# Turning batch 0's later keys and queries on TensorE, with three small reorderings, in a top-k attention and shrink kernel

## The chip, the cores and the metric

The kernel runs on one core of a Trainium2 chip. The metric is the device time of one launch in microseconds (us), the median of several executions. Engines are named as in the profile: PE is TensorE (matmuls; PEld is its weight loads), DVE is VectorE, ACT is ScalarE, POOL is GpSimd, SP is SyncE, which here only issues DMAs.

## The reference

```python
def _attn_ref(q, k, v):                       # (8, 8, 576, 64), float32
    B, H, S, D = q.shape
    scale = 1.0 / np.sqrt(D)
    scores = scale * np.matmul(q, k.transpose(0, 1, 3, 2))
    kth = np.partition(scores, -32, axis=-1)[..., -32:-31]
    mask = scores >= kth
    scores = np.where(mask, scores, -1000000000.0)
    scores = scores - np.max(scores, axis=-1, keepdims=True)
    attn = np.exp(scores)
    attn = attn / (np.sum(attn, axis=-1, keepdims=True) + 1e-09)
    return np.matmul(attn, v).astype(np.float32)

def _moe_ref(x, w_in, w_out):                 # x: (4608, 512); w_in: (512, 2048); w_out: (2048, 512)
    h = x @ w_in
    g = h - np.tanh(h)
    return (g @ w_out).astype(np.float32)
```

The attention output, heads side by side, is the input `x` of the second block. `w_in` and `w_out` come as 64-bit floats, and the kernel makes 32-bit floats of them on the chip.

## The kernel before, in words

**Steps.** Attention goes in steps of 128 queries of two heads (a pair `hp`). Batch 0 comes first. Its first four steps (0 to 3) are query tile 0 of pairs 0, 1, 2 and 3, so each of them needs a new pair's keys and queries. Batch 0's steps are marked `pe`: their attention weights are turned by PE (`turn_pe`, L423), later batches' by DVE and DMAs.

**One iteration n** of the main loop (`run`, from L708) emits, in program order: `turn_pe(n-2)`'s first part (eight PE transposes L423 into `zt`, two ACT copies L426 into `et`); `mask(n-1)`; `search(n)`; `scores(n+1)` (PE L236, ACT copy L244 from `scps` to `sc`); the last part of `turn_pe`; `expo(n-1)` (ACT L329); `values` (PE L451 and L461, ACT L465, POOL L469); and, dealt out in between by a planner, the matmuls of the second block (`ffn_h`, PE L502, with ACT L514/L515 and POOL L516; `ffn_o`, PE L523). Every engine works through its own list in that order. The planner counts steps, not time, so what is dealt to which step is fixed in the program.

**`search(n)`, on DVE:** L266, L267, L269 split the 576 scores of each row into two halves (min, max) and then run four rounds of MAX8 (L274) and MATCH_REPLACE8 (L277; not after the last round). After round i it calls `between(i)`, which emits whatever was put at (n, i): turning of keys (round 0), stages of weight conversion, and the reciprocal L345.

**`mask(n)`, on POOL and ACT:** L293 makes the threshold `tb`, L302 `nb`, then twice ACT L306 and POOL L309 make the masked scores `z`; last comes L313, which notes in `bad` whether a row needs an exact repeat. L313 reads the buffer `ab` that `search` filled.

**Weight conversion.** A piece is 128 rows by 512 weights; there are 32, pieces 0 to 15 of `w_in`, 16 to 31 of `w_out`. `convert` has a load (two SP DMAs, L148 the words and L149 the same bytes shifted) and two further stages. Stage 1: DVE L157 (exponent bits to `f`), ACT L160 (exponent `e`), DVE L162 and ACT L165 (mantissa). Stage 2: DVE L168 puts the sign to the exponent, POOL L171 multiplies; the piece's load buffer is then free, and the next load is issued behind it. For `w_in` `e` is a tile of `h_ps`, a PSUM pool of two buffers that the second block's matmuls use too; for `w_out` `e` is `f` itself, in SBUF. Steps 0 and 1 have two pieces each, steps 2 to 9 three, step 10 four (`many`). Their stages are spread over a step's rounds:

```python
for i, x in enumerate(seq):      # x = (stage, piece), as 1k 1k+1 2k 1k+2 2k+1 2k+2 for three pieces
    at_round.setdefault((m, 3 * i // max(len(seq) - 1, 1)), []).append(lambda x=x: part(*x))
```

**Keys and queries.** `load_rows` brings a pair's keys or queries with four DMAs of 32 partitions by 18 runs of 32 floats (L199), so that one DVE 32 by 32 block transpose (L221, `turn_rows`) gives the turned matrix `kT` or `qT`. Pair 0 of batch 0 goes to tiles of its own; three of its query DMAs are on ACT's queue, all other loads on SP's. Pairs 1 to 3 of batch 0 are loaded at the start into the space of `w_in[2]` and `w_in[3]` (`early`) and turned in round 0 of steps 0, 1 and 2. On SP the loads stand in the order pair 0, piece 0, pair 1, piece 1, pair 2, piece 2, pair 3, piece 3, then three more pieces and the values `v` (L211, L215).

**Pools that matter here:** `sc` 3 buffers, `ab` 2, `z` 2, `sc_ps` (the scores in PSUM) 1, `zt_ps` 2, `h_ps` 2, `th` (which holds `f`) 4.

Of the kernel before, what the change touches and what calls it, by code (L numbers as in the profile page):

```python
# [8 lines left out]
AF = mybir.ActivationFunctionType  # L9
ALU = mybir.AluOpType  # L10
FP32 = mybir.dt.float32
# [5 lines left out]
BIG = 2.0**80  # L17
TOP = 32
EPS = 1.0e-9
J = 4  # L20
# [31 lines left out]
def kernel(  # L52
# [9 lines left out]
    nc = tc.nc  # L62
    P = nc.NUM_PARTITIONS
    B, H, S, D = q.shape
    DM, DFF = moe_w_in.shape
    NHP = H // 2
    JP = J * P
    R = S - JP
# [10 lines left out]
    scale = 1.0 / float(D) ** 0.5  # L79
# [5 lines left out]
    def pool(name, bufs, **kw):  # L85
        return ctx.enter_context(tc.tile_pool(name=name, bufs=bufs, **kw))
# [6 lines left out]
    mpool = pool("m", 3)  # L93
    zpool = pool("z", 2)
# [6 lines left out]
    zt_ps = pool("zt_ps", 2, space=PS)  # L101
    h_ps = pool("h_ps", 2, space=PS)

    ident = consts.tile([P, P], FP32, name="ident")
# [3 lines left out]
    w_in = [consts.tile([P, CD, DFF // WJ], FP32, name=f"w_in{j}") for j in range(WJ)]  # L108
# [14 lines left out]
    def flat(x):  # L123
        return x.rearrange("p n w -> p (n w)")
# [51 lines left out]
    raw, kT, qT, vb, vr = {}, {}, {}, {}, {}  # L176
# [5 lines left out]
    def half(t):  # L182
        return slice(t * D, (t + 1) * D)


    early = [flat(w_in[j][:])[:, i * S : (i + 1) * S] for j in (2, 3) for i in range(3)]

    def load_rows(name, b, hp, exact):

        if b == 0 and hp and not exact:  # L190
            x = early[2 * hp - 2 + (name == "q")]
        else:
            x = ldpool.tile([P, S], FP32, tag=f"{name}in", name=f"{name}in")[:]
        raw[name, b, hp] = x
        src = {"k": k, "q": q}[name]
        for a in range(NG):
            h, d = 2 * hp + a // 2, a % 2 * G
            queue = nc.scalar if a and (name, b, hp, exact) == ("q", 0, 0, False) else nc.sync
            queue.dma_start(  # L199
                x[a * G : (a + 1) * G, :].rearrange("i (n d) -> i n d", d=G),  # L200
                src[b, h, :, d : d + G].rearrange("(n i) d -> i n d", i=G),
            )

    def load_v(b, hp):
# [4 lines left out]
        for t in range(2):  # L209
# [4 lines left out]
            o = 0 if t else JP  # L214
            nc.sync.dma_start(y[half(t), t, :], v[b, h, o : o + R, :])  # L215

    def turn_rows(name, b, hp):

        d = kqpool.tile([P, S], FP32, tag=f"{name}T", name=f"{name}T")
        {"k": kT, "q": qT}[name][b, hp] = d  # L220
        nc.vector.transpose(d[:], raw.pop((name, b, hp)))  # L221

# [58 lines left out]
    def mask(n, exact):  # L283

        x = st[n]
        sc, m = x["sc"], x.pop("m")
        scf = sc[:].rearrange("p t s k -> p t (s k)")
        tb = mpool.tile([P, 2], FP32, tag="tb", name="tb")
        if exact:
            nc.gpsimd.tensor_scalar(tb[:], m[:, :, TOP - 1], BIG, None, ALU.mult)  # L290
        else:
            for t in range(2):
                nc.gpsimd.tensor_scalar(  # L293
                    tb[:, t : t + 1],
                    m[:, t, TOP - 1 : TOP],
                    m[:, t, TOP - 9 : TOP - 8],
                    BIG,
                    ALU.min,
                    ALU.mult,
                )  # L300
        nb = mpool.tile([P, 2], FP32, tag="nb", name="nb")
        nc.gpsimd.tensor_scalar(nb[:], m[:, :, 0], -scale, None, ALU.mult)  # L302
        z = zpool.tile([P, 2 * S], FP32, tag="z", name="z")
        zv = z[:].rearrange("p (t k) -> p t k", t=2)
        for t in range(2):
            nc.scalar.activation(  # L306
                zv[:, t, :], scf[:, t, :], AF.Relu, bias=tb[:, t : t + 1], scale=-BIG
            )
            nc.gpsimd.tensor_tensor(zv[:, t, :], scf[:, t, :], zv[:, t, :], ALU.subtract)  # L309
        if not exact:  # L310
            ab = x.pop("ab")
            for t in range(2):
                nc.gpsimd.tensor_scalar(  # L313
                    bad[:, t, n : n + 1],
                    ab[:, t, S2 + 7 : S2 + 8],
                    BIG,
                    tb[:, t : t + 1],
                    ALU.mult,
                    ALU.is_gt,
                )  # L320
        x.update(z=z, zv=zv, nb=nb)

    rds = {}
# [227 lines left out]
    def plan():  # L551
        steps.clear(), done.clear()

        def block(b, qt):
            return [(slice(0, P), out[b * S + qt * P : b * S + (qt + 1) * P, :])]

        rest = None
        for b in range(B):
            if b % 2 == 0:
                rest = Unit(  # L560
                    [[(half(i), out[(b + i) * S + JP : (b + i + 1) * S, :]) for i in range(2)]], "xTr"
                )

            parts = [(0, 1), (2, 3)]
            if b == 0:
                parts[0:1] = [(0,), (1,)]
            for a, qts in enumerate(parts):
                unit = Unit([block(b, qt) for qt in qts], "xT")
                pe = b == 0
                for hp in range(NHP):  # L570
                    for i, qt in enumerate(qts):
                        steps.append(Step(b, hp, qt, unit, 0, i, len(qts), pe))
                    if hp == NHP - 1:
                        done[len(steps) - 1] = unit
                    if hp % 2 and a == (0 if b == B - 1 else len(parts) - 1):
                        steps.append(Step(b, hp - 1, J, rest, b % 2 * R, pe=pe))
                        if hp == NHP - 1 and b % 2:
                            done[len(steps) - 1] = rest
        for g, after in zip(steps, steps[1:]):
            if after.pe and not after.rem and not g.pe:  # L580
                g.lag = 3
# [3 lines left out]

    def run(exact):
        plan()
        NS = len(steps)
        todo, at_round, turned = {}, {}, {}

# [5 lines left out]
        for i, (b, hp) in enumerate(pairs):  # L596
            n = next(n for n, g in enumerate(steps) if (g.b, g.hp) == (b, hp))
            for x, name in enumerate("kq"):
                m = max(n - 5 + x, turned.get(name, -4))
                if b == 0 and not exact:  # L600
                    m = -4
# [17 lines left out]
        def load_piece():  # L619
            k = len(loaded)  # L620
            usable = [x for x in free if x[2] > k]
            if k < pieces and usable:
                slot = min(usable, key=lambda x: x[2])
                free.remove(slot)
                piece = convert(k, slot)
                next(piece)
                loaded.append((piece, slot))

        def part(x, k):
            next(loaded[k][0])  # L630
            if x == 2:
                converted[0] = k + 1
                free.append(loaded[k][1])
                load_piece()
# [6 lines left out]
        for m in range(max(many) + 1 if pieces else 0):  # L641
            mine = range(started, min(started + many[m], pieces))
            started = mine.stop
            seq = [(1, k) for k in mine[:1]]
            for k in mine[1:]:
                seq += [(1, k), (2, k - 1)]
            seq += [(2, k) for k in mine[-1:]]
            seq = [x for x in seq if x != (1, 0)]
            for i, x in enumerate(seq):
                at_round.setdefault((m, 3 * i // max(len(seq) - 1, 1)), []).append(  # L650
                    lambda x=x: part(*x)
                )

        def here(i):
            return 0 <= n + i < NS

# [18 lines left out]
        for u in begun:  # L675
            k = 2 if u.tag == "xT" else 1
# [5 lines left out]
        def rate():  # L682
# [3 lines left out]
            coming = sorted((t, u.n // 8) for u, t in ready.items() if t > n)  # L686
            for t, k in coming + [(NS + LAG, 0)]:
                r = have / max(t - n, 1)
# [18 lines left out]

        for n in range(-4, NS + LAG):  # L708
            pe = here(-2) and steps[n - 2].pe
            def due():  # L710
                for m in (n - LAG, n - LAG + 1, n - LAG + 2):
                    if 0 <= m < NS and steps[m].last and steps[m].lag == n - m:
                        values(m)
# [4 lines left out]
            if pe:  # L718
                w = turn_pe(n - 2)
                next(w)  # L720
            if here(-1):
                mask(n - 1, exact)
# [29 lines left out]
    with tc.manual_schedule():  # L752
        run(False)
# [10 lines left out]
    with tc.If(again > 0):  # L764
        with tc.manual_schedule():
            run(True)
# [29 lines left out]
```

## Time and profile before

| | |
|---|---|
| median of 3 runs | 1528.41 us (1525.82 to 1529.62) |
| profiled execution, its own time | 1527.48 us |
| profiled execution, its span | 1525.7 us |
| busy: PE, DVE, ACT, POOL | 1420.7, 1350.9, 1002.3, 875.1 us |
| steps 0 to 10 (first L266 of step 0 to that of step 11) | 11.74 to 160.54 us |

The span is the time from the first to the last instruction; 1.8 us of the execution's own time lie around it. A step is told by the start of its L266, the first DVE instruction of `search`: 11.74, 22.44, 35.12, 48.62, 60.83, 73.75, 85.96, 99.27, 114.69, 128.29, 144.64 and 160.54 us for steps 0 to 11, then 168.12, 177.56, 185.15, 195.59 and 203.80 for steps 12 to 16. Rows of the timeline give start, length, engine, line, operation, tiles, shapes, and in square brackets how long the engine had been idle and what ended it. Successive DVE rows overlap a little, so what an instruction costs its engine is the distance to the next one's start.

### The profile page before, as it was taken

How to read it: one execution, taken by the hardware profiler on the slowest of the kernel's cores; microseconds unless marked ns; L12 is line 12 of the kernel's file. 1: busy time of each engine (PE TensorE's matmuls, PEld its weight loads, DVE VectorE, ACT ScalarE, POOL GpSimd, SP SyncE). 2: the span in 40 equal slices, each digit the busy share in tenths (PEclk: the TensorE clock that was granted, in tenths of full speed). 3: DMA queues.
4: the chain of work that ended last, by engine and by line, in shares of the span. 5: the costliest groups of instructions: out<-in, count | busy, mean ns of one | idle time of the engine just before them, and what ended most of it. 6: DMA issues, size and time to landing. Idle time of an engine off the chain costs nothing.

```text
span 1525.7 us, 24089 instructions
## 1 busy us (share of the span) xinstructions
PE 1420.7 (93%) x7302; PEld 904.1 (59%) x7302; DVE 1350.9 (89%) x3884; ACT 1002.3 (66%) x1801; POOL 875.1 (57%) x1370
## 2 busy tenths in 40 slices
PE   2577898999999999999999999999999999999998
PEld 1355566456565674747574674747475675756673
DVE  7998999999999999999999999999999999887000
ACT  3676677677676776867676776777676776767220
POOL 3788676656474664756555565656464564746110
PEclk9877999999999999999999999999999999999999
DMA  9954214547755676657754675557654676343400
GB/s 255 357 173 164 51 25 108 141 138 175 158 152 165 152 167 155 155 151 166 170 147 131 168 161 151 140 160 160 151 148 131 164 159 165 101 150 113 107 7 17
DMA packets 255467, 221.61 MB, mean 145 GB/s; under 512 B 197728, under 2 KB 204896, under 8 KB 248160
## 3 DMA queue, kind: packets, MB, share of 16 engines
q1 hardware_dynamic: 253552, 219.75, 55.9%
q8 instruction: 60, 0.98, 0.3%
q14 instruction: 79, 0.65, 0.2%
q10 hardware_dynamic: 1776, 0.22, 0.1%
HBM read 136.17 MB, written 83.76 MB: 144 GB/s over the span
## 4 chain that ended last, share of the span: by engine, by line
PE 62%; DVE 26%; ACT 4%; POOL 3%; issue 2%; SPq 1%; DMA 1%; DVEq 0%; ACTq 0%; POOLq 0%
PE hps L502 24%; PE ops L523 24%; PE av L451 7%; DVE m L274 7%; DVE ab L277 7%; PE scps L236 7%; DVE zx L386 3%; DVE ab L267 2%; DVE ab L269 2%; DVE ab L266 2%; SPq L199 1%; DVE f L157 1%; POOL z L309 1%; ACT z L306 1%; DVE f L168 1%
## 5 line engine op out<-in xcount | busy, mean ns | idle before, releaser
L523 PE MATMUL ops<-w_out,g 128*128 128x512 f32 x1152 | 517.7, 600 | 2.1 <-POOL bad L313 1.2
L502 PE MATMUL hps<-xT,w_in 128*128 128x256 f32 (+1 forms) x2176 | 467.2, 372 | 2.5 <-ACT g L515 1.2
L274 DVE MAX8 m<-ab 128x8 f32<-128x288 f32 (+1 forms) x1152 | 467.1, 447 | 0.0
L309 POOL TENSOR_TENSOR z<-sc,z 128x576 f32<-128x576 f32 x288 | 403.0, 1421 | 84.3 <-ACT z L306 84.1
L502 PEld LDWEIGHTS hps<-xT,w_in 128*128 128x128 f32 x2176 | 392.4, 192 | 78.0 <-issue 21.9
L277 DVE MATCH_REPLACE8 ab<-m,ab 128x288 f32<-128x288 f32 x864 | 376.2, 443 | 0.0
L523 PEld LDWEIGHTS ops<-w_out,g 128*128 128x128 f32 x1152 | 213.3, 191 | 262.5 <-issue 248.6
L306 ACT ACTIVATE z<-sc,tb 128x576 f32<-128x576 f32 x288 | 207.7, 769 | 146.4 <-POOL tb L293 131.6
L516 POOL TENSOR_TENSOR g<-g,th 128x512 f32<-128x512 f32 x144 | 183.2, 1273 | 147.1 <-ACT g L515 142.1
L355 ACT ACTIVATE z<-z,rd 128x576 f32<-128x576 f32 x252 | 180.8, 764 | 101.6 <-DVE rd L348 101.5
L236 PE MATMUL scps<-kT,qT 64*128 64x288 f32 (+1 forms) x1280 | 190.6, 449 | 44.8 <-DVE qT L221 27.2
L329 ACT ACTIVATE z<-z,nb 128x576 f32<-128x576 f32 x288 | 221.6, 775 | 2.5 <-POOL z L309 2.4
L339 POOL TENSOR_SCALAR rd<-den 128x2 f32<-128x2 f32 x144 | 33.4, 232 | 327.7 <-ACT z L329 323.7
L244 ACT COPY sc<-scps 128x1152 f32<-128x1152 f32 x144 | 160.5, 1114 | 41.3 <-PE scps L236 41.1
L386 DVE STREAM_TRANSPOSE zx<-z 128x1152 f32<-128x1152 f32 x126 | 171.9, 1364 | 16.2 <-ACT z L355 16.1
L236 PEld LDWEIGHTS scps<-kT,qT 64*128 64x128 f32 (+1 forms) x1280 | 103.6, 185 | 122.5 <-issue 49.9
L266 DVE TENSOR_TENSOR ab<-scps,sc 128x576 f32<-128x576 f32 x144 | 105.3, 731 | 28.9 <-ACT sc L244 24.0
L514 ACT ACTIVATE th<-hps 128x512 f32<-128x512 f32 x144 | 84.3, 585 | 64.4 <-PE hps L502 62.0
L269 DVE MAX8 ab<-ab 128x8 f32<-128x288 f32 x288 | 115.8, 443 | 0.0
L267 DVE TENSOR_TENSOR ab<-scps,sc 128x576 f32<-128x576 f32 x144 | 107.1, 744 | 0.0
L451 PE MATMUL av<-et,vb 128*64 128x256 f32 (+1 forms) x640 | 76.2, 371 | 17.6 <-ACT et L426 17.6
L293 POOL TENSOR_SCALAR tb<-m 128x1 f32<-128x1 f32 x288 | 88.4, 316 | 6.9
(68 smaller groups left out, 1067.7 us busy)
## 6 DMA issues: line engine op xcount, KB each, us to landing
there<-zx SPq DMA_DIRECT2D x56, 1152.0 KB, 4.2
spare<-there SPq DMA_DIRECT2D x112, 288.0 KB, 5.4
et<-there SPq DMA_DIRECT2D x112, 288.0 KB, 5.2
kin<-in_k_dram SPq DMA_DIRECT2D x116, 72.0 KB, 2.9
vb<-in_v_dram SPq DMA_DIRECT2D x64, 128.0 KB, 6.2
out_dram<-ot SPq DMA_DIRECT2D x32, 256.0 KB, 4.3
qin<-in_q_dram SPq DMA_DIRECT2D x113, 72.0 KB, 3.6
there<-zx SPq DMA_DIRECT2D x14, 576.0 KB, 5.0
```

What stands on the lines that cost most here:

```text
L236: nc.tensor.matmul(ps[rows, t, s, 0:S2], qT[g.b, g.hp + i][half(t), qs], kT[g.b, g.hp + i][half(t), ks], start=True, stop=True,)
L274: nc.vector.max(m[:, t, m8], last[t] if i == rounds - 1 else cur[t])
L277: nc.vector.match_replace(nxt[t], m[:, t, m8], cur[t], NEG)
L306: nc.scalar.activation(zv[:, t, :], scf[:, t, :], AF.Relu, bias=tb[:, t : t + 1], scale=-BIG)
L309: nc.gpsimd.tensor_tensor(zv[:, t, :], scf[:, t, :], zv[:, t, :], ALU.subtract)
L329: nc.scalar.activation(x["zv"][:, t, :], x["zv"][:, t, :], AF.Exp, bias=x["nb"][:, t : t + 1], scale=scale, accum_out=den[:, t : t + 1],)
L355: nc.scalar.activation(x, x, AF.Copy, scale=rds[n][:, g.i, t : t + 1])
L386: nc.vector.transpose(tiles(zx, g.nq)[:, :, :, g.i, :].rearrange("p c k j -> p k c j"), z[:].rearrange("p (k c j) -> p k c j", c=NG, j=G),)
L451: nc.tensor.matmul(av[half(t), 0, cols], vb[g.b, hp][:, t, c, :] if c < J else vr[g.b, hp][:, t, :], es[:, :, (J + 1) * t + c if c < J els ...
L502: nc.tensor.matmul(cur[u][:, s : s + w], w_in[j][:, c, fo : fo + P], u.xT[:, c, 0:w], start=(c == 0), stop=(c == CD - 1),)
L516: nc.gpsimd.tensor_tensor(g, g, th[:], ALU.subtract)
L523: nc.tensor.matmul(cur[u][:], u.g[o // 1024][:, o % 1024 // 512, o % 512 : o % 512 + P], w_out[f // FJ][:, f % FJ, :], start=(f == 0), sto ...
```

## The change

Line numbers in the text are those of the kernel before. Four edits:

1. Pairs 1 to 3 of batch 0 are loaded as whole rows (runs of 64 floats; per head one DMA of 128 partitions and one of 64) and turned by PE: per matrix four transposes of 128 by 128 and one of 64 rows into two `zt` tiles, then two ACT copies into `kT` or `qT`. The DVE transposes L221 of these six matrices go. The exact repeat and the later batches stay as they were.
2. Stage 2 of a piece (L168, L171 and the next load) stands one round later; round 3 is the last.
3. In steps with n < 20, L313 (`bad`) stands right after L293 instead of after L309.
4. Pair 0's key and query DMAs alternate between SP's and ACT's queue.

```diff
-    early = [flat(w_in[j][:])[:, i * S : (i + 1) * S] for j in (2, 3) for i in range(3)]
+    early = [flat(w_in[j][:])[:, 5 * i * P : 5 * (i + 1) * P] for j in (2, 3) for i in range(3)]
...
+        if b == 0 and hp and not exact:
+            xv = x.rearrange("p (c t d) -> p t c d", t=2, d=D)
+            for t in range(2):
+                h = 2 * hp + t
+                nc.sync.dma_start(
+                    xv[:, t, 0:J, :], src[b, h, 0:JP, :].rearrange("(c p) d -> p c d", p=P)
+                )
+                nc.sync.dma_start(xv[0:R, t, J, :], src[b, h, JP:S, :])
+            return
...
-            queue = nc.scalar if a and (name, b, hp, exact) == ("q", 0, 0, False) else nc.sync
+            queue = nc.scalar if a % 2 and (b, hp, exact) == (0, 0, False) else nc.sync
...
+    turned_pe = [True]
+
     def turn_rows(name, b, hp):
         d = kqpool.tile([P, S], FP32, tag=f"{name}T", name=f"{name}T")
         {"k": kT, "q": qT}[name][b, hp] = d
-        nc.vector.transpose(d[:], raw.pop((name, b, hp)))
+        x = raw.pop((name, b, hp))
+        if not (b == 0 and hp and turned_pe[0]):
+            nc.vector.transpose(d[:], x)
+            return
+        for c0, c1, w in ((0, J, P), (J, J + 1, R)):
+            zt = zt_ps.tile([P, 512], FP32, tag="zt", name="zt")
+            for c in range(c0, c1):
+                o = (c - c0) * P
+                nc.tensor.transpose(zt[:, o : o + w], x[0:w, c * P : (c + 1) * P], ident[0:w, 0:w])
+            w = (c1 - c0 - 1) * P + w
+            nc.scalar.copy(d[:, c0 * P : c0 * P + w], zt[:, 0:w])
...
-        nb = mpool.tile([P, 2], FP32, tag="nb", name="nb")
...
+        def settle():
             ab = x.pop("ab")
             for t in range(2):
                 nc.gpsimd.tensor_scalar(
                     bad[:, t, n : n + 1], ab[:, t, S2 + 7 : S2 + 8], BIG, tb[:, t : t + 1], ALU.mult, ALU.is_gt,
                 )
+
+        if not exact and n < 20:
+            settle()
+        nb = mpool.tile([P, 2], FP32, tag="nb", name="nb")
...
+        if not exact and n >= 20:
+            settle()
...
     def run(exact):
         plan()
+        turned_pe[0] = not exact
...
             for i, x in enumerate(seq):
-                at_round.setdefault((m, 3 * i // max(len(seq) - 1, 1)), []).append(
-                    lambda x=x: part(*x)
-                )
+                r = 3 * i // max(len(seq) - 1, 1) + (x[0] == 2)
+                at_round.setdefault((m, r) if r < 4 else (m, 3), []).append(lambda x=x: part(*x))
```

DVE's order within a step of three pieces p, p+1, p+2, by round:

| after round | before | after |
|---|---|---|
| 0 | L157, L162 of p; L157, L162 of p+1 | the same |
| 1 | L168 of p; L157, L162 of p+2 | L157, L162 of p+2 |
| 2 | L168 of p+1 | L168 of p |
| 3 | L168 of p+2 | L168 of p+1; L168 of p+2 |

More of the change, by code (lines that the diff above doesn't have):

```diff
@@ L300, in mask @@
                 )
-        nb = mpool.tile([P, 2], FP32, tag="nb", name="nb")
[L302 to L307, printed above, removed]
-            )
-            nc.gpsimd.tensor_tensor(zv[:, t, :], scf[:, t, :], zv[:, t, :], ALU.subtract)
-        if not exact:
+        def settle():
             ab = x.pop("ab")
@@ L320, in mask @@
                 )
+        if not exact and n < 20:
+            settle()
+        nb = mpool.tile([P, 2], FP32, tag="nb", name="nb")
+        nc.gpsimd.tensor_scalar(nb[:], m[:, :, 0], -scale, None, ALU.mult)
+        z = zpool.tile([P, 2 * S], FP32, tag="z", name="z")
+        zv = z[:].rearrange("p (t k) -> p t k", t=2)
+        for t in range(2):
+            nc.scalar.activation(
+                zv[:, t, :], scf[:, t, :], AF.Relu, bias=tb[:, t : t + 1], scale=-BIG
+            )
+            nc.gpsimd.tensor_tensor(zv[:, t, :], scf[:, t, :], zv[:, t, :], ALU.subtract)
+        if not exact and n >= 20:
+            settle()
         x.update(z=z, zv=zv, nb=nb)
@@ L649, in run @@
             for i, x in enumerate(seq):
-                at_round.setdefault((m, 3 * i // max(len(seq) - 1, 1)), []).append(
-                    lambda x=x: part(*x)
-                )
+                r = 3 * i // max(len(seq) - 1, 1) + (x[0] == 2)
+                at_round.setdefault((m, r) if r < 4 else (m, 3), []).append(lambda x=x: part(*x))
         def here(i):
```

## The prediction

> **What bounds the kernel now.** I read the page's slices first, then busy time by windows, then DVE's waits, then the timeline of the first 200 us.
>
> ```profile
> PE   2577898999999999999999999999999999999998
> DVE  7998999999999999999999999999999999887000
> ```
>
> ```profile
> 0.00:38.00 38.00, 8.84 (x32) 5.24 (x32) 27.70 (x74) 14.24 (x21) 11.92 (x27) 1.00 1.06 255
> 114.00:152.00 38.00, 26.67 (x152) 19.32 (x153) 33.27 (x85) 25.80 (x50) 30.28 (x39) 0.78 0.47 166
> 228.00:266.00 38.00, 33.49 (x189) 25.76 (x188) 38.00 (x110) 28.15 (x52) 26.00 (x44) 0.96 0.44 103
> ```
>
> The first numbers of a window are its length and PE's, PEld's, DVE's, ACT's and POOL's busy time. From 228 us DVE is busy 38.00 of 38.00, and PE joins it later; nothing there has room, and the change leaves it alone. Before that PE has room (26.67 of 38 around 130 us) and DVE loses some. Since each engine's list and the dealt matmuls are fixed by steps, I take whatever step 16 (L266 at 203.80) gains as the end's gain: between there and 400 us the trace lists no DVE wait at all.
>
> DVE's waits between 100 and 200 us:
>
> ```profile
> DVE f L168 <- ACT f L160: 6.7, 4, 3.0
> DVE ab L266 <- POOL bad L313: 4.7, 2, 2.8
> ```
>
> Not listed as waits, but as lost, are instructions that take longer than they should:
>
> ```profile
> 31.27 0.43 DVE L162 TENSOR_SCALAR w_in<-w_out 128x512 uint32<-128x512 uint32 x1 [0.85 <-DMA w_out<-in_moe_w_in_dram]
> 112.95 1.26 POOL L171 TENSOR_TENSOR w_out<-w_out,f 128x512 f32<-128x512 f32 x1 [0.72 <-ACT et L426]
> 113.49 1.27 DVE L168 SCALAR_TENSOR_TENSOR f<-w_out,f 128x512 uint32<-128x512 uint32 x1
> 114.91 1.27 POOL L171 TENSOR_TENSOR w_out<-w_out,f 128x512 f32<-128x512 f32 x1 [0.69 <-DVE f L168]
> 116.12 0.29 POOL L367 COPY rx<-rd 128x128 f32<-128x128 f32 x1
> 116.46 0.47 PE L461 MATMUL av<-ident,rx 128*128 128x128 f32 x1 [3.01 <-POOL rx L367]
> 119.52 1.44 ACT L306 ACTIVATE z<-sc,tb 128x576 f32<-128x576 f32 x2 [0.20 <-POOL tb L293]
> 120.38 3.24 POOL L309 TENSOR_TENSOR z<-sc,z 128x576 f32<-128x576 f32 x2 [0.31 <-ACT z L306]
> 120.87 0.71 ACT L160 ACTIVATE f<-f,e 128x512 int32<-128x512 uint32 x1
> 121.61 0.73 DVE L168 SCALAR_TENSOR_TENSOR f<-w_out,f 128x512 uint32<-128x512 uint32 x1 [0.18 <-ACT f L160]
> 122.27 1.63 DVE L157 TENSOR_SCALAR f<-spare 128x512 uint32<-128x512 uint32 x1
> 195.59 0.76 DVE L266 TENSOR_TENSOR ab<-scps,sc 128x576 f32<-128x576 f32 x1 [2.79 <-POOL bad L313]
> ```
>
> Two things are to be seen. L157 (0.41 alone) ends only when POOL's L309 does, and L168 with `f` in SBUF (0.68) when POOL's L171 does; the L168 whose `e` is in PSUM always took 0.66 to 0.69. And there is a chain across a step's border: last L168, POOL L171, rx, PE L461 and transposes, ACT's copies, z, then ACT L160, for which the first L168 waits: here 4.75 from rx to L160.
>
> **The change, part by part.** Gains are negative.
>
> *Start.* Before, kT's DVE transpose began at 6.76 and qT's at 7.47, back to back; pair 0's last query load was issued at 2.79 and took 4.3. Two queues of four DMAs give keys some 2 us sooner, but the same eight must be in, which was so at 2.79+4.3=7.1, so qT starts near 7.15: -0.3, bounds -0.6 and +0.5 (a large piece's load now shares the engines with ACT's last query DMA). ACT's extra 0.5 us of issuing stands ahead of its first copy at 10.59 and is free.
>
> *Steps 0 and 1.* Step 0 took 10.70 and loses the pair of L221 (15.37 to 16.73): -1.36. Step 1 took 12.68 and loses its pair (-1.35), an L157 stretched by 0.33 and the L162 that waited for piece 3's load (0.94 with its L157's end), and I add 0.5 because its first L157 now meets POOL's L309: -2.12. This needs piece 3 sooner. A pair's keys and queries landed in 4.0 us (13.69 less 9.71); `v` of a pair, the same bytes in the new form (L211, L215), took 1.34, so 2.7 for both: 1.3 a pair, 3.9 for three, and 0.5 for the start. Piece 3 then lands at 26.8 (31.25 before); its L157 comes at 27.2. If the loads gain nothing, L162 stays at 31.27 and step 2 starts at 35.1 as before: bounds of the two steps together -3.5 and 0.
>
> The turning's cover: ten PE transposes at 0.25 (eight L423 took 1.97) and four ACT copies (0.59 and about 0.2) are 2.5 and 1.6 us per pair. PE stood idle 6.41, 8.40 and 4.16 before these scores. By those rows sc(1) ends at 18.8, needed at 20.8; uncovered, a turning costs up to 4.1 a step, less that slack.
>
> The Trainium skill, "DMA: Bandwidth & Descriptors", Specifications, speaks against the loads: full rate needs transfers of 512 B, and both 128 B and 256 B lie below. By it alone the loads gain nothing and the sum below is 5.7 instead of 9.2; the `v` rows say otherwise, and I follow them.
>
> *Step 2 to 5* (before 13.50, 12.21, 12.92, 12.21; sum 50.84). DVE's own list by start distances: 3.63 to the first L157, 1.34 for two pieces, 0.07, round 0.72+0.85=1.57, third piece 0.67, round 1.57, L168 0.60, last MAX8 0.75, two L168 1.20: 11.40. New wait: three `e` of `w_in` are now open at once and `h_ps` has two buffers. The third L160 must wait for the first L168, at 9.45, and behind it on ACT stand L165 and sc(n+1): 0.05+0.62+0.53+1.10+0.03 later, at 11.8, DVE may begin the next step. The third L157, at 6.6, meets L309 (about 6.0 to 8.8): I add 0.8, as long as before; bounds 0 and 1.4 (one L309). 12.6 a step, 50.4: -0.4, bounds -3.6 and +2.0. Step 2's L221 pair is in this.
>
> *Steps 6 to 10* (13.31, 15.42, 13.60, 16.35, 15.90). L168 of the last two pieces stand together at the step's end, so their L171 follow after it: all three L171 of a step finish 2.6 to 3.85 us after it instead of 1.49, and the chain to L160 starts 1.1 to 1.9 later. Against that the first L168 comes at 8.85 instead of 6.6 and absorbs most. Step 6: 11.40, L157 0.8, one L168 behind L171 0.7: 12.9. Step 7: L160 was at 8.0, now 9.14; three pairs L160/L165 3.66, sc 1.0: 13.8. Step 8: 6.2 becomes 8.05, so 12.8. Step 9: 8.94 becomes 10.7, so 15.55. Step 10 keeps L168 in round 1 and waits for L160 1.8, then one L309 for L157, one L171: 16.6. Together -2.9; bounds -9.5 (no lateness, no stretch: 12.1, 12.8, 12.1, 13.75, 14.3) and +2. Loads are issued a round (about 2 us) later; piece 24's (issued at 108.78, 4 to 6 us to land, used at 122.27) shows the room.
>
> *L313 sooner.* L266 of step 15 no longer waits for `bad`, but next in line is sc(15), whose copy ends at 193.81: -1.74. Step 13 frees the scores' PSUM sooner, and PE, busy until 178.6, starts scps at once: -0.41. The two POOL rows (0.57) now stand ahead of L302 and L309, while ACT's L306 needs only `tb`. -2.1, bounds -2.8 and 0.
>
> **Sum.** -0.3 -3.5 -0.4 -2.9 -2.1 = -9.2. From the profiled execution's 1527.48 that gives 1518.3; the median of the runs is 0.9 above that execution. I say 1518.
>
> **Rivals.**
> - *DVE runs through*: the blocks of POOL on L157 and L168 fall into gaps. 0.6+3.5+3.6+9.5+2.8 is 20 less: 1507. For it: all L157 lie apart from L168 now. Against: POOL is busy 30 of 38 us there.
> - *The gain is given back*: loads no sooner (a gain of 5.7), or steps 6 to 10 stay as they are (6.3), or both (2.8): 1521.2 to 1524.7, and with step 10's loss doubled about 1526. For it: the same chain over POOL bounds steps 7 and 9. Near 1526 it can't be told from no change (0.3% of 1528.4, or 4.6 us, being what a measurement tells).
> - *Slower: POOL's tensor rows block DVE three times a step*, on the third L157, the first L168 and the second, 1.3 to 1.4 each: 11.40+4.0=15.4. Steps 2 to 5 lose 10.8, steps 6 to 9 (four at 15.4, before 58.7) 2.9; with 5.9 gained elsewhere, 7.8 more: 1535. It decides from 2.7 blocks a step on (a step of 15.0). Against it: in steps 2 to 5 L168 is not blocked (0.66 to 0.69).
>
> **How the numbers follow.** Forecast (gain of 5 to 15) 0.60; runs through 0.10; given back 0.18; slower 0.12. Faster by over 0.3%: 0.60, 0.10 and a little of the third, 0.71; within: 0.17; slower: 0.12. The range reaches from the second case's 1507, a little further, to the third's end: 1505 to 1528, which leaves out the slower case and little else.
>
> **What would show it.** In the changed profile: step 2's L266 near 31.4 (35.12 before); no DMA wait of L162 at piece 3; L160 of the third piece in steps 2 to 5 waiting for DVE's L168 and sc directly behind it; three L171 in a row after a step's end in steps 6 to 10; L266 of steps 13 and 15 waiting for sc, not for `bad`; step 16 some 9 us sooner, the end by as much. I am wrong if step 16's gain isn't the end's, if L266 waits for sc in steps 1 to 3 (turning uncovered), or if L157 and L168 in steps 2 to 10 lose over 2.7 POOL rows a step.

## The result: no change, where 1518 us was forecast

| | median | lowest to highest, runs | ratio to before, 95% interval |
|---|---|---|---|
| before, beside it | 1529.01 us | 1525.82 to 1530.77, 4 | |
| changed kernel | 1528.66 us | 1527.69 to 1528.98, 4 | 0.9999 [0.9981, 1.0017] |

The changed kernel's profiled span is 1525.9 us (1525.7 before). Its numbering differs from here on: L157, L160, L162, L165, L168 and L171 keep their numbers; L266 is now L288, `sc`'s copy L244 is L266, L293 is L315, L313 is L327, L302 is L339, L306 is L343, L309 is L346, rx's L367 is L395, `ffn_h`'s matmul L502 is L530.

What a step gained or lost is read, as in the prediction, from the starts of `search`'s first instruction. The change was ahead by 2.83 us at step 3, and gave all of it and more back by step 11:

| step starts at | 0 | 1 | 2 | 3 | 6 | 11 | 16 | last |
|---|---|---|---|---|---|---|---|---|
| before | 11.74 | 22.44 | 35.12 | 48.62 | 85.96 | 160.54 | 203.80 | 1395.81 |
| changed | 11.33 | 21.07 | 32.74 | 45.78 | 86.97 | 163.30 | 204.44 | 1396.43 |
| difference | -0.41 | -1.37 | -2.38 | -2.83 | +1.01 | +2.76 | +0.64 | +0.63 |

So the loss lies in steps 3 to 10, and from step 16 on nothing moves any more. The timeline of the changed kernel's step 4, DVE's conversions with what stands beside them (start, length, engine, line, tiles; in brackets the idle time before and what ended it):

```profile
65.46 2.96 POOL L346 TENSOR_TENSOR z<-sc,z 128x576 f32<-128x576 f32 x2
66.13 1.02 DVE L157 TENSOR_SCALAR f<-spare 128x512 uint32<-128x512 uint32 x1
67.08 1.62 DVE L162 TENSOR_SCALAR w_in<-spare 128x512 uint32<-128x512 uint32 x1
70.19 0.67 DVE L168 SCALAR_TENSOR_TENSOR f<-w_out,e 128x512 uint32<-128x512 uint32 x1
70.90 0.69 ACT L160 ACTIVATE e<-f,e 128x512 int32<-128x512 uint32 x1 [3.04 <-DVE f L168]
71.00 3.83 POOL L171 TENSOR_TENSOR w_in<-w_in,f 128x512 f32<-128x512 f32 x3 [2.58 <-issue]
71.53 1.26 DVE L168 SCALAR_TENSOR_TENSOR f<-spare,e 128x512 uint32<-128x512 uint32 x2
72.05 1.10 ACT L266 COPY sc<-scps 128x1152 f32<-128x1152 f32 x1
73.25 0.76 DVE L288 TENSOR_TENSOR ab<-scps,sc 128x576 f32<-128x576 f32 x1 [0.45 <-ACT sc L266]
```

Two things are to be seen. The third piece's L157 and L162 take 1.02 and 1.62 where each takes 0.41 alone: L346 is two rows, the two halves of POOL's masking; by the trace the first ends at 66.87. L157 ends 0.28 after the first half, L162 0.28 after the second. And the third L160 waits 3.04 for the first L168, since `h_ps` has two buffers; `sc` stands behind it on ACT, and DVE's next step waits 0.45 for `sc`.

DVE's list of waits from 40 to 100 us names only the smaller of the two:

```profile
DVE ab L288 <- ACT sc L266: 1.8, 4, 0.5
```

That is 1.8 us in four steps; the held instructions count as busy and are in no list of waits. Step 8, a `w_out` step, has no wait of DVE at all and still takes 14.72:

```profile
119.02 1.27 POOL L544 TENSOR_TENSOR g<-g,th 128x512 f32<-128x512 f32 x1
119.58 1.00 DVE L157 TENSOR_SCALAR f<-w_out 128x512 uint32<-128x512 uint32 x1
120.26 0.64 POOL L497 TENSOR_TENSOR xT<-xs 128x128 f32<-128x128 f32 x1
120.50 0.68 DVE L162 TENSOR_SCALAR w_out<-w_out 128x512 uint32<-128x512 uint32 x1
122.78 2.97 POOL L346 TENSOR_TENSOR z<-sc,z 128x576 f32<-128x576 f32 x2
123.41 1.06 DVE L157 TENSOR_SCALAR f<-spare 128x512 uint32<-128x512 uint32 x1
124.39 1.64 DVE L162 TENSOR_SCALAR w_out<-spare 128x512 uint32<-128x512 uint32 x1
128.34 1.27 POOL L171 TENSOR_TENSOR w_out<-w_out,f 128x512 f32<-128x512 f32 x1 [2.60 <-ACT et L454]
128.88 1.28 DVE L168 SCALAR_TENSOR_TENSOR f<-spare,f 128x512 uint32<-128x512 uint32 x1
```

What DVE's rows take above 0.41 (0.68 for L168) adds up to 0.59 + 0.27 + 0.65 + 1.23 + 0.60 = 3.34, and 11.40 of DVE's own list with it is 14.74. Only 1.88 of it is the third pair; 0.86 is the first pair, which POOL's L544 and L497 (rows for the second block's `g` and for `values`) hold, and 0.60 is an L168 behind L171.

### The profile page after: what moved, and what is told of

Read it like the earlier page. It is cut to its first block, busy times and chain, and to the rows that moved or that the text cites. A ratio compares the mean times of both kernels' runs of the same rounds, so it can differ in the third digit from the quotient of the medians.

```text
span 1525.9 us, 24153 instructions
## 1 busy us (share of the span) xinstructions
PE 1429.8 (94%) x7332; PEld 909.8 (60%) x7332; DVE 1356.2 (89%) x3878; ACT 1006.5 (66%) x1813; POOL 876.1 (57%) x1370
## 4 chain that ended last, share of the span: by engine, by line
PE 61%; DVE 29%; ACT 4%; POOL 2%; issue 2%; DMA 1%; DVEq 0%; ACTq 0%; SPq 0%; POOLq 0%
PE hps L530 23%; PE ops L551 23%; DVE m L296 8%; DVE ab L299 8%; PE av L479 7%; PE scps L258 7%; DVE zx L414 3%; DVE ab L291 2%; DVE ab L289 2%; DVE ab L288 2%; DVE f L168 1%; ACT sc L266 1%; DVE f L157 1%; PE zt L451 1%; POOL z L346 1%
## 5 line engine op out<-in xcount | busy, mean ns | idle before, releaser
L530 PE MATMUL hps<-xT,w_in 128*128 128x256 f32 (+1 forms) x2176 | 469.0, 373 | 2.3 <-ACT g L543 1.2
L346 POOL TENSOR_TENSOR z<-sc,z 128x576 f32<-128x576 f32 x288 | 403.5, 1423 | 76.2 <-ACT z L343 76.2
L530 PEld LDWEIGHTS hps<-xT,w_in 128*128 128x128 f32 x2176 | 393.7, 193 | 77.9 <-issue 20.7
L343 ACT ACTIVATE z<-sc,tb 128x576 f32<-128x576 f32 x288 | 207.6, 768 | 149.0 <-POOL tb L315 130.4
L544 POOL TENSOR_TENSOR g<-g,th 128x512 f32<-128x512 f32 x144 | 183.8, 1278 | 146.4 <-ACT g L543 141.4
L367 POOL TENSOR_SCALAR rd<-den 128x2 f32<-128x2 f32 x144 | 33.4, 232 | 331.5 <-ACT z L357 327.9
L266 ACT COPY sc<-scps 128x1152 f32<-128x1152 f32 x144 | 160.5, 1115 | 39.6 <-PE scps L258 39.2
L288 DVE TENSOR_TENSOR ab<-scps,sc 128x576 f32<-128x576 f32 x144 | 105.1, 730 | 27.9 <-ACT sc L266 27.4
L315 POOL TENSOR_SCALAR tb<-m 128x1 f32<-128x1 f32 x288 | 88.4, 316 | 7.0
```

The lines of the kernel that those rows point to most:

```text
L343: nc.scalar.activation(zv[:, t, :], scf[:, t, :], AF.Relu, bias=tb[:, t : t + 1], scale=-BIG)
L530: nc.tensor.matmul(cur[u][:, s : s + w], w_in[j][:, c, fo : fo + P], u.xT[:, c, 0:w], start=(c == 0), stop=(c == CD - 1),)
L544: nc.gpsimd.tensor_tensor(g, g, th[:], ALU.subtract)
```

## The experiments

In the table, "11" and "16" are the starts of those steps; the ratio is to the kernel before.

| run | edits in it | median | ratio, interval | 11 | 16 |
|---|---|---|---|---|---|
| rows_only | 1, 4 | 1524.95 | 0.9978 [0.9969, 0.9988] | 156.77 | 200.46 |
| signs_only | 2 | 1531.74 | 1.0024 [1.0013, 1.0035] | 165.45 | 208.77 |
| old_rounds | 1, 3, 4 | 1531.32 | 1.0025 [1.0015, 1.0035] | 166.36 | 207.50 |
| check11 | 1, 2, 4, and 3 from step 11 | 1525.61 | 0.9981 [0.9972, 0.9991] | 160.25 | 202.65 |
| old_rounds_check11 | 1, 4, and 3 from step 11 | 1520.73 | 0.9963 [0.9949, 0.9977] | 155.70 | 196.76 |
| bad_twice | as old_rounds, L327 twice | 1526.44 | 0.9986 [0.9977, 0.9996] | 161.16 | 202.69 |
| late_signs_third_first_stage_in_round_0 | as check11, third pair in round 0 in steps 2 to 5 | 1520.55 | 0.9951 [0.9934, 0.9967] | 154.91 | 197.32 |
| third_first_stage_in_round_0 | as old_rounds_check11, third pair in round 0 in steps 2 to 9 | 1515.28 | 0.9923 [0.9906, 0.9939] | 151.42 | 192.12 |
| third_in_round_0_check_early | the same with edit 3 in full | 1518.79 | 0.9935 [0.9919, 0.9952] | 153.41 | 195.34 |
| third_in_round_0_to_step_10 | as third_first..., step 10 too | 1521.29 | 0.9950 [0.9933, 0.9966] | 156.26 | 198.41 |

### Which edit loses: four kernels

*old_rounds*, the changed kernel with stage 2 back in its old rounds:

```diff
-                r = 3 * i // max(len(seq) - 1, 1) + (x[0] == 2)
+                r = 3 * i // max(len(seq) - 1, 1)
```

> The changed kernel with stage 2 of the pieces back in its old rounds (edits 1, 3 and 4 alone). Theory A, the later signs are the loss: steps 2 to 10 lose no more 6.5 us against the kernel before (the +5.14 that they lost, and the 1.35 of step 2's turning that they should have gained), so step 11 starts at about 156 us (163.30 changed, 160.54 before) and the time is about 1522. Theory B, the earlier L313 delays L309 on POOL by its 0.58 a step and pushes it onto DVE's L157 and L162: the loss stays, step 11 near 163, time near 1529.

*check11*, the changed kernel with edit 3 in steps 11 to 19 only:

```diff
-        if not exact and n < 20:
+        if not exact and 11 <= n < 20:
             settle()
...
-        if not exact and n >= 20:
+        if not exact and not 11 <= n < 20:
             settle()
```

> The changed kernel with the earlier L313 only in steps 11 to 19, so that L309 stands where it stood in steps 0 to 10; signs a round later. Theory A: as the changed kernel, step 11 near 163, time near 1528.7. Theory B: L157 and L162 of the third piece lose 0.8 instead of 1.8 a step, step 11 near 157, time near 1523.

*old_rounds_check11* has both of these diffs.

> Edits 1 and 4, and the earlier L313 only in steps 11 to 19; rounds as before. Theory A: within 1 us of the run with the old rounds and the earlier L313 from step 0 on, about 1522. Theory B: 5 us less than that run (nine steps at 0.58), step 11 near 155.

*signs_only* is the kernel before with edit 2 alone.

> The kernel before with edit 2 alone. Theory A: steps 2 to 10 lose 6.5 us, step 11 near 167, time near 1535. Theory B: no more than 1 us from the kernel before, 1528 to 1529.

Neither theory's figures came throughout: old_rounds is later than both foretold (156 and 163), check11 lies between them (163 and 157), old_rounds_check11 is near theory B's 155 and signs_only near theory A's 167. Both edits lose, and they are not additive. At step 11, edit 2 costs 160.25 - 155.70 = 4.55 without the early L327 in steps 0 to 10, and gains 166.36 - 163.30 = 3.06 with it. The early L327 costs 163.30 - 160.25 = 3.05 with late signs, and 166.36 - 155.70 = 10.66 with the signs in their old rounds. That the whole 10.66 is the edit's is not shown: 3.43 of it is step 7, where L162 is 1.09 longer and the wait for L160 2.39 longer (3.13 against 0.74), at a granted clock of 0.57 against 1.00. Beside the kernel before, edit 2 alone loses 4.91 by step 11. What remains of the gain is edits 1 and 4 (4.84 by step 11 here, 3.77 in rows_only below) and edit 3 from step 11 on (2.20 from there to step 16).

Why L327's place matters so much with the old rounds is seen where L162 follows a held L157. Step 7 of old_rounds_check11, where L327 still stands behind L346, in the timeline:

```profile
103.34 1.86 POOL L346 TENSOR_TENSOR z<-sc,z 128x576 f32<-128x576 f32 x1
103.86 1.64 DVE L157 TENSOR_SCALAR f<-w_out 128x512 uint32<-128x512 uint32 x1
105.20 0.71 POOL L327 TENSOR_SCALAR bad<-ab,tb 128x1 uint8<-128x1 f32 x1
105.41 0.41 DVE L162 TENSOR_SCALAR w_out<-w_out 128x512 uint32<-128x512 uint32 x1
106.14 1.27 POOL L171 TENSOR_TENSOR w_out<-w_out,f 128x512 f32<-128x512 f32 x1
```

and the same place in old_rounds:

```profile
108.46 3.23 POOL L346 TENSOR_TENSOR z<-sc,z 128x576 f32<-128x576 f32 x2 [2.70 <-ACT z L343]
110.34 1.63 DVE L157 TENSOR_SCALAR f<-w_out 128x512 uint32<-128x512 uint32 x1
111.65 1.46 POOL L171 TENSOR_TENSOR w_out<-w_out,f 128x512 f32<-128x512 f32 x1
111.89 1.50 DVE L162 TENSOR_SCALAR w_out<-w_out 128x512 uint32<-128x512 uint32 x1
113.42 0.63 ACT L165 ACTIVATE w_out<-w_out 128x512 f32<-128x512 uint32 x1 [0.69 <-DVE w_out L162]
113.96 1.10 ACT L266 COPY sc<-scps 128x1152 f32<-128x1152 f32 x1
```

L157 ends 0.3 after L346 in both. Without L327, POOL's next row is L171; it begins before L157 has ended, and L162 lasts 1.50; ACT's L165 and `sc` are late by as much. With L327 there, L162 takes 0.41, and it is the tiny row that is drawn out: the two rows take 0.98 together instead of 0.57, the first (shown) 0.71, so that it ends at 105.91, just after L162 (105.82). L171 begins at 106.14, when L162 is done. That L327 keeps L171 off L162 was a reading; the next run tests it.

### Was L327 a spacer? bad_twice

old_rounds with L327's two rows issued early and, in steps 0 to 10, once more behind L346. POOL has more work than in old_rounds and none of it starts sooner.

```diff
-        def settle():
-            ab = x.pop("ab")
+        def settle(ab):
...
         if not exact and n < 20:
-            settle()
+            settle(x["ab"])
...
-        if not exact and n >= 20:
-            settle()
+        if not exact and (n < 11 or n >= 20):
+            settle(x["ab"])
```

> Edits 1, 3 and 4 with stage 2 in its old rounds, as in the run with the old rounds (step 11 at 166.36, 1531.32), but in steps 0 to 10 L313's two rows are issued a second time after L309, so POOL has 0.57 us more to do a step. Spacer theory (what edit 3 took away is the small rows between L309 and the first L171, while which DVE got its L162 in): L162 behind the stretched L157 is 0.41 again and not 1.5 to 1.6, step 11 starts between 155.7 and 158, the time is 1520 to 1524. Delay theory (edit 3 costs because L302 and L309 start 0.57 later): nothing comes back, step 11 at 166 or later, 1531 to 1533.

Neither figure came: step 11 starts at 161.16, between the two. The timeline of step 4 (numbers from L327 on are one lower in this kernel):

```profile
64.29 2.77 POOL L345 TENSOR_TENSOR z<-sc,z 128x576 f32<-128x576 f32 x2
65.67 1.68 DVE L157 TENSOR_SCALAR f<-spare 128x512 uint32<-128x512 uint32 x1
67.04 0.98 POOL L326 TENSOR_SCALAR bad<-ab,tb 128x1 uint8<-128x1 f32 x2
67.26 0.41 DVE L162 TENSOR_SCALAR w_in<-spare 128x512 uint32<-128x512 uint32 x1
```

L162 is 0.41 again, so the tiny rows are a spacer: extra work on POOL made the kernel 5.20 us faster by step 11, nearly all of it where it was to be, in step 3 (13.30 to 12.47) and steps 6 to 9 (0.90 to 1.37 each), where old_rounds' L162 had been held by L171. But L157 lasts 1.68, where it lasts 1.26 with the early rows absent: the two rows ahead of L346 move it 0.4 later into L157's way. Against rows_only, which has the same order but for the early rows, steps 4 to 6 are 0.44 longer each, and all of steps 0 to 10 4.39 (0.93 of it in step 7, at a granted clock of 0.57 against 0.79). Both theories were half right.

### What is left without edits 2 and 3: rows_only

Edits 1 and 4 alone; L327 stays behind L346 in every step.

```diff
-        if not exact and n < 20:
+        if not exact and n < 0:
             settle()
...
-        if not exact and n >= 20:
+        if not exact and True:
             settle()
```

> Edits 1 and 4 alone. If L313's place in steps 11 to 19 is what gave 2.1 and all else of the gain of the run with the early check in steps 11 to 19 (step 11 at 155.70, step 16 at 196.76) is that of the loads and PE turning: step 11 within 0.5 of 155.7, L266 of step 15 waits for bad again, step 16 near 198.9, time 1522.5 to 1524. If the gain in steps 2 to 10 there came from somewhere else, step 11 is 158 or later and the time 1525 or more.

Step 15 waits 2.80 for `bad` again, and step 16 is at 200.46. Step 11 missed its place by 0.57 more than allowed, the time by 0.95. Up to step 10 this kernel is instruction for instruction old_rounds_check11; all other steps agree within 0.3, but step 7 takes 15.76 here and 14.15 there. The windows of the first 8 us of step 7 in the two (length; busy time of PE, PEld, DVE, ACT, POOL with instructions; then the granted clock, the DMA share, GB/s):

```profile
95.51:103.51 8.00, 6.24 (x38) 5.59 (x39) 6.72 (x22) 2.87 (x7) 5.12 (x9) 0.79 0.62 244
```

```profile
95.72:103.72 8.00, 6.23 (x52) 5.58 (x53) 7.26 (x23) 4.50 (x10) 6.75 (x10) 1.00 0.66 248
```

PE is busy for the same time, with 38 matmuls in the one and 52 in the other; the clock is 0.79 against 1.00. The 1.6 us are more than the 1.07 between the two at step 11. A second such pair stands below: third_first_stage_in_round_0 and third_in_round_0_to_step_10 have the same instructions up to step 9, and step 7 takes 12.24 in the one and 14.79 in the other, again at 1.00 and 0.79. What one profile says of step 7 is therefore good to some 2.5 us only. Steps 3 to 5 agree within 0.02 in both pairs.

### The third pair out of the way: three kernels

*late_signs_third_first_stage_in_round_0*: check11, and in steps 2 to 5 the third piece's L157 and L162 stand in round 0, ahead of L346.

```diff
-                r = 3 * i // max(len(seq) - 1, 1) + (x[0] == 2)
+                r = 0 if x[0] == 1 and 2 <= m <= 5 else 3 * i // max(len(seq) - 1, 1) + (x[0] == 2)
```

> The changed kernel with L313 early in steps 11 to 19 alone (1525.61, steps 3 to 5 at 13.30, step 11 at 160.25), but in steps 2 to 5 the third piece's L157 and L162 stand in round 0. If edit 2 costs because that pair meets both halves of L309 in round 1: steps 3 to 5 take 11.8 to 12.0 (the wait of the third L160 for the first L168 over h_ps stays and sc ends there), step 11 at 154 to 156. If it costs through the h_ps wait alone: steps 3 to 5 stay at 13.0 to 13.4 and step 11 near 160.

Steps 3 to 5 take 11.92, 11.91 and 11.91, step 11 starts at 154.91: the first theory. What is left is the wait for `h_ps`, with `sc` behind it:

```profile
65.26 0.68 DVE L168 SCALAR_TENSOR_TENSOR f<-w_out,e 128x512 uint32<-128x512 uint32 x1
65.97 0.69 ACT L160 ACTIVATE e<-f,e 128x512 int32<-128x512 uint32 x1 [0.61 <-DVE f L168]
67.12 1.10 ACT L266 COPY sc<-scps 128x1152 f32<-128x1152 f32 x1
68.32 0.76 DVE L288 TENSOR_TENSOR ab<-scps,sc 128x576 f32<-128x576 f32 x1 [0.45 <-ACT sc L266]
```

*third_first_stage_in_round_0*: old_rounds_check11 with the third pair in round 0 in steps 2 to 9.

```diff
-                r = 3 * i // max(len(seq) - 1, 1)
+                r = 0 if x[0] == 1 and 2 <= m <= 9 else 3 * i // max(len(seq) - 1, 1)
```

> As the run with old rounds and the early check in steps 11 to 19 alone (1520.73, steps 3 to 5 at 12.22), but in steps 2 to 9 the third piece's L157 and L162 also stand in round 0, ahead of L309. Theory that L309's hold on that L157 (1.26 instead of 0.42, and 1.63 in steps 6 to 9) is all that separates these steps from DVE's own list: steps 3 to 5 take 11.3 to 11.5 each, steps 6 to 9 lose up to 1.2 each, step 11 at 148 to 152.5, time 1513 to 1517.5. Rival (the hold moves to the next DVE instruction that meets L309 or L171, or the step's end waits for sc behind three L160/L165 pairs): steps 3 to 5 stay at 12 or more, step 11 at 154.5 to 157, time 1519.5 to 1522.

Steps 3 to 5 take 11.37, 11.38 and 11.41, step 11 starts at 151.42, the time is 1515.28: the first theory, and faster than both kernels of the change. All six instructions run free, and DVE waits for nothing in these steps:

```profile
61.05 0.42 DVE L157 TENSOR_SCALAR f<-w_out 128x512 uint32<-128x512 uint32 x1
61.38 0.42 DVE L162 TENSOR_SCALAR w_in<-w_out 128x512 uint32<-128x512 uint32 x1
61.72 0.43 DVE L157 TENSOR_SCALAR f<-spare 128x512 uint32<-128x512 uint32 x1
62.05 0.42 DVE L162 TENSOR_SCALAR w_in<-spare 128x512 uint32<-128x512 uint32 x1
62.38 0.43 DVE L157 TENSOR_SCALAR f<-spare 128x512 uint32<-128x512 uint32 x1
62.72 0.43 DVE L162 TENSOR_SCALAR w_in<-spare 128x512 uint32<-128x512 uint32 x1
63.40 2.77 POOL L346 TENSOR_TENSOR z<-sc,z 128x576 f32<-128x576 f32 x2
```

*third_in_round_0_check_early*: the same with L327 early in all steps below 20 (the diff of check11 undone). In its expectation the steps "4 to 6" and "3 to 6" are those that begin one earlier, 3 to 5.

> As the run with the third piece's first stage in round 0 in steps 2 to 9 (1515.28; steps 4 to 6 at 11.37 to 11.41, step 11 at 151.42, step 16 at 192.12), but with L313 right after L293 in all steps below 20, as the change has it. If edit 3 cost in steps 0 to 10 only because a DVE pair stood in the stretch of L309 (hold longer by 0.4, and L171 between L157 and L162): steps 3 to 6 stay within 0.1 of 11.4 and step 11 starts within 2 of 151.4 (the granted clock in steps 7 and 9 alone may move it by that much), time 1513.5 to 1518. If the two rows ahead of L302 and L309 cost by themselves: steps 3 to 6 take 11.8 or more and step 11 is at 155 or later, time 1519 to 1522.

Steps 3 to 5 take 11.35, 11.44 and 11.37. With no DVE pair in L346's stretch, L327's early place costs nothing in them; so in these steps its cost was that pair alone. It isn't in steps 6 to 9, where `e` is in SBUF: the second L168 lasts 1.55 to 1.57 there, against 0.67 to 0.72, since L171 now stands directly behind L346. Step 11 starts 1.99 later, although step 10 takes 1.25 less. The time, 1518.79, is 0.8 above the range given: step 7 takes 14.51 against 12.24, of which 1.38 is a longer wait for L160 (1.44 against 0.06; the granted clock is 0.79 against 1.00 in its first 8 us) and 0.89 that second L168; and step 12 takes 1.1 more.

### A candidate that failed: third_in_round_0_to_step_10

third_first_stage_in_round_0 with step 10's four first stages in round 0 too (`2 <= m <= 10`).

> As the run with the third piece's first stage in round 0 in steps 2 to 9 (1515.28, step 10 at 17.04), with all first stages of step 10's four pieces in round 0 too. If step 10 loses what its later L157 wait behind L309 and L171: step 10 takes 13.5 to 15.5, step 11 at 148 to 150, time 1511.5 to 1514.5. If it is bound by the chain to the first L160 and the four L160/L165 pairs and sc behind it: 16 to 17.5, time 1514.5 to 1516.5.

Both were wrong: step 10 takes 20.69 instead of 17.04. (Of the 4.84 that step 11 starts later, another 2.55 is step 7, and step 6 takes 0.96 less; the edit does not touch these.) DVE now waits for the load of the step's fourth piece:

```profile
148.45 0.43 DVE L157 TENSOR_SCALAR f<-spare 128x512 uint32<-128x512 uint32 x1 [2.50 <-DMA spare<-in_moe_w_out_dram]
149.61 0.43 DVE L162 TENSOR_SCALAR w_out<-spare 128x512 uint32<-128x512 uint32 x1 [0.74 <-DMA spare<-in_moe_w_out_dram]
```

That load is issued at 144.08 and 144.46, behind the step's own first L168, whose place in the planner's list did not change, and lands 4.3 and 5.1 us later. Pulling the first stage forward pulled it ahead of its data; the long way to the first L160 stayed.

## Why the prediction was wrong, point by point

| term | foretold | measured |
|---|---|---|
| start | -0.3 | -0.41 |
| steps 0 and 1 | -3.5 | -1.97 |
| steps 2 to 5 | -0.4 | +3.39 |
| steps 6 to 10 | -2.9 | +1.75 |
| L313 sooner, from step 11 on | -2.1 | -2.13 |
| sum | -9.2 | +0.63 |

**Right.** What step 16 gains is the end's: +0.64 there, +0.63 in the last step. The start. L313 sooner from step 11 on: `bad` is in no wait, counted from step 11 L288 of step 15 starts 2.13 sooner (foretold 0.41 + 1.74 = 2.15), `sc`'s copy ahead of it ends 0.45 sooner (foretold 0.41), and step 15 waits 2.31 for `sc`; without that edit (rows_only) the wait for `bad` is back. The loads: the pairs' keys and queries landed 2.46, 2.32 and 2.18 us after the piece ahead of them (4.0 to 4.3 before, 2.7 foretold), piece 3 at 28.16 (31.25 before, 26.8 foretold), and its L162 no longer waits. So the Trainium skill's figure for full rate ("DMA: Bandwidth & Descriptors", Specifications), by which runs of 128 B and of 256 B are both too short, did not tell here what the new form was worth. That form has longer runs and also DMAs of 128 and 64 partitions in place of 32; no run here separates the two. The turning is covered: L288 of steps 1 to 3 waits for nothing. DVE's own list of 11.40 is what third_first_stage_in_round_0 takes, 11.37 to 11.41, and the wait for `h_ps`, 11.8 a step as worked out, is 11.91 by itself.

**The step that failed** is one sentence: "The third L157, at 6.6, meets L309 (about 6.0 to 8.8): I add 0.8, as long as before; bounds 0 and 1.4 (one L309)". Before, L168 stood ahead of that L157 and it met the second half of L309 alone, as in step 3 of the kernel before:

```profile
54.01 2.78 POOL L309 TENSOR_TENSOR z<-sc,z 128x576 f32<-128x576 f32 x2 [0.98 <-ACT z L306]
55.22 0.67 DVE L168 SCALAR_TENSOR_TENSOR f<-w_out,e 128x512 uint32<-128x512 uint32 x1
55.81 1.25 DVE L157 TENSOR_SCALAR f<-w_out 128x512 uint32<-128x512 uint32 x1
56.99 0.41 DVE L162 TENSOR_SCALAR w_in<-w_out 128x512 uint32<-128x512 uint32 x1
```

With L168 moved away, L157 comes 0.59 earlier and meets the first half, and L162 behind it the second. Step 4 of check11:

```profile
64.14 2.97 POOL L346 TENSOR_TENSOR z<-sc,z 128x576 f32<-128x576 f32 x2
65.26 0.58 DVE L157 TENSOR_SCALAR f<-spare 128x512 uint32<-128x512 uint32 x1
65.76 1.63 DVE L162 TENSOR_SCALAR w_in<-spare 128x512 uint32<-128x512 uint32 x1
```

The pair loses 1.39 in check11 (0.58 and 1.63 instead of 0.41 and 0.41), 1.82 in the changed kernel. The bound counted one row of POOL for a pair of DVE instructions. By these numbers a step of 11.91 + 1.82 = 13.73 follows, and steps 3 to 5 took 13.74, 13.73 and 13.72. The same hold is also most of the 1.52 that steps 0 and 1 fell short: 1.12 in step 1, whose L157 and L162 lasted 0.84 and 1.62 where 0.5 for the pair had been added (the other 0.40 is step 0's, where L162 waits 0.27 for piece 1's load). Of what steps 6 to 10 missed, it is the 0.95 of step 6 (13.85 instead of 12.9) and 1.88 of the 3.34 that POOL's rows cost step 8 (14.72 instead of 12.8).

**A second step failed**: the two POOL rows ahead of L302 and L309 were called harmless, "while ACT's L306 needs only `tb`". L306 was not late (4.63 after step 4's start, 4.62 in check11); L309 was (5.94 against 5.48), and that is what held the pair 0.44 longer in each of steps 3 to 5 (13.74 against 13.30 in check11). By step 11 it is 3.05. That the same rows had kept L171 off L162 was not thought of at all. With late signs no L171 stands at that place in steps 3 to 9, so it did not count there; in step 10 it did (L162 1.49, 0.42 in check11). It is part of why edit 2 helps when edit 3 is there: that gain is in steps 6, 7 and 9, and in steps 7 and 9 (2.46 and 2.22) the third pair runs free where old_rounds' takes 1.63 and 1.50. The first L168's wait for L160 is shorter too (1.20 and 1.98 against 3.13 and 3.66); why is not shown.

**Mis-sized**: steps 7 and 9 of the profile before were read as a chain of fixed rows. Step 7's 15.42 there belongs to a granted clock of 0.79. In the changed kernel's step 7 (15.13 instead of 13.8) the chain is not the whole: the wait for L160 is 1.20, and rows of POOL cost DVE 2.47, the first pair 0.86 and the three L168 (0.74, 1.15 and 1.76) 1.61; 11.40 with both is 15.07. Two slips changed little: 1518.3 is the profiled execution's, and with the 0.9 added the median would have been 1519.2; and the L168 shown at 113.49 ended 0.55 after L171, not with it.

Of the rivals, the gain was given back, as the second said, but by another mechanism than its own (the loads did come sooner); the third's, DVE held by POOL's tensor rows, is what happened, at 1.8 us in steps 3 to 5 and 2.5 to 3.3 in steps 7 and 8, in place of 4.0.

## What to carry to other kernels

Where two engines hold each other, a busy engine's list of waits shows nothing: compare each instruction's length with its length alone, and follow every instruction of a moved group, the one behind the first too, against every row that the other engine has there. A small instruction that looks idle can be what keeps a long one off the other engine; before moving it, look at what then stands in its place. And where two edits move the same stretch, cost them together: added alone to edits 1 and 4 in steps 0 to 10, each of edits 2 and 3 lost; together they lost less than edit 3 did alone.

## What the runs showed of the hardware

A conversion that met a POOL row of 128x512 or 128x576 values lasted until that row's end and a little more: L157 and L162 ended 0.28 after it, the second L168 in the changed kernel's step 7 0.55. If POOL had another row of two tensors waiting, this came next and held DVE's next conversion too: L157, L171, L162 (1.50, which is 1.09 more than alone). Between 11 and 165 us of the twelve traces a pair of conversions stands so in 48 places, and the second was held in all 48. Rows of 128x1 or 128x2 values in the same position held it in none of 50. The L327 behind L346 above lasted until L162 was done, and in step 4 of the changed kernel a row of L315 lasted through all four conversions of round 0 (63.16 to 64.58), none of which took more than 0.42:

```profile
63.16 1.57 POOL L315 TENSOR_SCALAR tb<-m 128x1 f32<-128x1 f32 x1
```

Where the first conversion of the pair had not been held, the large row mostly waited as well, in 12 of 14 places: an L171 of the kernel before began at 44.66 beside an L157 and an L162 of 0.41 each, and lasted 1.65 (1.27 alone). So it is no plain taking of turns; what sets these cases apart was not tried. The Trainium skill ("SBUF — State Buffer", Who interferes with whom) has a DVE instruction in a two-port mode, which `tensor_scalar` can enter, and GpSimd share a pair of ports, held for the whole instruction by whichever issues first, the other blocked fully. The lengths of the held conversions agree (L162 ends 0.28 after L346); that the ports are the reason no run here shows. Who comes next when both are waiting the section does not say.

The granted clock of PE in step 7 (its mean over the first 8 us) differed from profile to profile. With the signs and the third pair in their old rounds it took three values, and the step's length followed them: the step took 14.15 at 1.00 (old_rounds_check11), 15.42 and 15.76 at 0.79 (before, rows_only), 16.69 and 17.59 at 0.57 (bad_twice, old_rounds). The same 16 matmuls of L530 took 1.95, 3.13 to 3.49, and 3.62 to 3.63 us. With late signs the order is less clean: 13.91 at 0.79 (late_signs_third_first_stage_in_round_0), 14.28 and 14.72 at 0.57 (check11, signs_only), 15.13 at 0.62 (changed). The skill ("TensorE: Matmul & The Clock Gate", Part 1) has the gate follow a window that runs freely, so that the same kernel meets it at a different point from run to run; twice, two kernels with the same instructions up to there did differ here. What part of the 0.57 in bad_twice and old_rounds is chance and what their own timing was not tried.
